# Regrouped first loads and an earlier start of pair 0 in an attention and mixture-of-experts kernel

## Chip, cores and metric

The kernel runs on one core of one Trainium2 chip. The metric is the device time of one execution in microseconds; the median of several executions is compared.

## What is computed

Four batches of eight heads of causal attention over 768 tokens with head size 64, and on its output a soft mixture of experts with 8 experts of 4 slots each. A head is either a retrieval head (full causal attention) or a streaming head (4 sink tokens and a window of 64); which one it is comes in as data.

```
scores = q @ k.T / 8                            # per batch and head, 768 x 768
keep   = causal & (retrieval | sink | window)   # sink: column < 4, window: row - column < 64
a      = softmax(where(keep, scores, -1e9));  x = a @ v
x      -> (3072, 512)                           # tokens x (heads * head size)
logits = x @ phi                                # 3072 x 32 slots
slot_input = softmax over tokens(logits).T @ x
slot_out[e] = relu(slot_input[e] @ w1[e]) @ w2[e]     # 512 -> 1024 -> 512, 8 experts
out    = softmax over slots(logits) @ slot_out  # 3072 x 512, float32
```

## The kernel before

The attention part works on 16 pairs of heads, numbered n = 0 to 15: pair n is heads 2(n mod 4) and the next one of batch n // 4. The schedule is written out by hand: each engine runs its instructions in the order of the program, and waits by semaphore for what they need.

**One pair.** `load` (L70) brings q, k and v with a cast from float32 to bfloat16, 96 partitions with 8 rows of 64 each. `transpose` (L80) turns each with 16 PE transposes into PSUM, `evac` (L89) copies that to SBUF (pair 0's q on ACT, all others on DVE); for v a second set of transposes, `v_blocks`, and `evac_blocks` build the layout for the second product. The causal scores are cut into six groups, g = 0 to 5 (`GROUPS`, L23). For each, `qk` (L113) makes the scores on PE and the exponential on ACT; `mask` (L134) multiplies groups 0 to 2 by the head's mask on DVE; the sink and window rule of groups 3 to 5 is a bias (`fb0`, `fb1`) inside the exponential. `pvmm` (L145) multiplies by v on PE, `norm` divides on DVE. Two PSUM tiles hold scores at a time. While pair n is in groups 2, 3 and 4, the q, k and v of pair n + 1 are transposed and copied. `x_transpose`, `token_logits`, `exp_tokens`, `exp_slots` and `dispatch` do the routing of a batch while the next batch's attention runs.

**Raw tiles.** The q, k and v that were loaded wait in memory that belongs to the last three experts' second weights (`at.late = w2s[NE - 3:]`). `raw_tile` (L64) gives pair n its place: four places each for q, k and v, two couples of pairs. A load into a place must wait until PE has transposed what lies there, and those last weights must wait until pair 15 has been transposed.

**Loads.** GpSimd (POOL) issues nearly all of them on one queue, q0, in the order of the program: k and v of pair 0, q, k, v of pair 1, and q, k, v of pairs 2 and 3 in one load each; then, in the loop, one weight matrix of 1 MB per pair (none where n mod 4 is 3), and for odd n q, k, v of pairs n + 3 and n + 4. Behind n = 13 the rest follows: the last two second weights come in four halves of 512 KB, because the end is cut in two halves of the output's columns. q of pair 0 comes as float32 over SP and is cast by DVE and ACT (L368, L369).

**Start of pair 0.** Behind a few constants come the transposes of q and k with zero matmuls between them (`warm`, L58), whose results are not used. Then DVE reads the heads' flags (`rne`, `r1`, `r0`, L377 to L379) and makes the masks: `head_mask(h)` (L381) writes the mask of one head in two instructions. Heads 0 and 1 are made inside pair 0's group 0, the others at the places of `MASK_AT` (L33).

**End.** `layer1` makes the hidden layer of four experts at a time, `layer2(e, c0, cl)` (L543, matmul in L547) adds one expert's output, on half the columns for the last two experts. `row_sums(b)` (L240) makes the softmax's divisor of a batch. `slot_cols` (L572) scales, and `piece` (L580) makes and stores the output: first the first half of the columns for batches 0 and 1, then the second half, then batches 2 and 3 whole. Ahead of the expert layers five small loads on SP write a few values of `moe_phi` into the mask of head 7, which nothing reads any more (L480 to L482).

Of the kernel before, what the change touches and what calls it, by code (L numbers as in the profile page):

```python
# [10 lines left out]
F32 = mybir.dt.float32  # L11
BF16 = mybir.dt.bfloat16
I32 = mybir.dt.int32
ALU = mybir.AluOpType
# [15 lines left out]
MCOL = [0, None, 256]  # L30
NG = len(GROUPS)

MASK_AT = {(0, 2): 2, (0, 3): 3, (0, 4): 4, (1, 1): 5, (1, 2): 6, (1, 3): 7}  # L33


class Attn:
# [26 lines left out]

    def raw_tile(self, w, n):  # L64

        t = self.late["qkv".index(w)].rearrange("p (i h a) d -> p i h (a d)", i=2, h=4)[:, n // 2 % 2]
        self.rawt[w, n] = t[:, 2 * (n % 2):2 * (n % 2) + 2]
        return t

    def load(self, n, which="qkv", pairs=1):  # L70
        b, h = n // 4, 2 * (n % 4)
        for w in which:
            for m in range(n, n + pairs):
                t = self.raw_tile(w, m)
            c = 2 * (n % 2)
            self.nc.gpsimd.dma_start(  # L76
                t[:96, c:c + 2 * pairs],
                self.src[w][b, h:h + 2 * pairs].rearrange("h (p s) d -> p h (s d)", s=8))

    def transpose(self, n, w):  # L80
        src = self.rawt[w, n]
# [7 lines left out]
    def evac(self, n, w):  # L89
        tp = self.tp.pop((w, n))  # L90
        pool = self.vTp if w == "v" else self.qkT
        dst = pool.tile([P, 768], BF16, tag=w + "T", name=w + "T")
        o = dst.rearrange("c (j s p) -> c j s p", j=6, s=8)
        i = tp.rearrange("c (s j p) -> c j s p", j=6, s=8)
        if n == 0 and w == "q":
            self.nc.scalar.copy(o, i)
        else:
            self.nc.vector.tensor_copy(o, i)  # L98
        self.T[w, n] = dst
# [150 lines left out]
def kernel(  # L250
# [13 lines left out]
    nc = tc.nc  # L264
    B, H, S, D = q.shape
    n_sink, window = int(n_sink), int(window)
    ES = moe_phi.shape[1]
    NE, DM, F = moe_w1.shape
    SPE = ES // NE
    NP = B * H // 2  # L270
# [26 lines left out]
    fb0 = singles.tile([P, H], F32, name="fb0")  # L297
    fb1 = singles.tile([P, H], F32, name="fb1")
# [4 lines left out]
    with ExitStack() as actx:  # L303
# [5 lines left out]
        msk = asing.tile([P, H, 640], BF16, name="msk")  # L309
        ri = asing.tile([P, 2 * H], I32, name="ri")  # L310
        rne = asing.tile([P, H, 2], F32, name="rne")
        r1 = asing.tile([P, H], F32, name="r1")
        r0 = asing.tile([P, H], F32, name="r0")
# [8 lines left out]
                   fb0=fb0, fb1=fb1, vbufs=vbufs, scale=1.0 / (D ** 0.5))  # L322
        ir32 = is_retrieval.tensor.reshape([H]).bitcast(I32)
        at = Attn(nc, tc, actx, q, k, v, env)
# [14 lines left out]
        nc.gpsimd.memset(ident, 1.0)  # L339
        nc.gpsimd.affine_select(ident, ident, pattern=[[-1, P]], compare_op=ALU.is_equal,  # L340
                                fill=0.0, base=0, channel_multiplier=1)
        at.load(1)
        at.load(2, pairs=2)

        for vb in vbufs:
            nc.vector.memset(vb[:, :, :, 64:65], 1.0)
# [23 lines left out]
        at.transpose(0, "q")  # L370
        at.warm(4, 512)
        at.evac(0, "q")
        at.transpose(0, "k")
        at.warm(3, 512)
        at.evac(0, "k")

        nc.vector.tensor_single_scalar(rne, ri.rearrange("p (h c) -> p h c", c=2), 0.0, op=ALU.not_equal)  # L377
        nc.vector.tensor_tensor(r1, rne[:, :, 0], rne[:, :, 1], op=ALU.max)
# [2 lines left out]
        def head_mask(h):  # L381
            for c0, c1, r in ((0, 256, r0), (256, 640, r1)):
                nc.vector.tensor_scalar(msk[:, h, c0:c1], level[:, c0:c1], r[:, h:h + 1], 2.0,
                                        op0=ALU.add, op1=ALU.is_ge)

        for n in range(NP):
            if n % 2 and n + 3 < NP:
                at.load(n + 3, pairs=2)
            for _ in range(0 if n % 4 == 3 or n > 13 else len(w_order) - 5 if n == 13 else 1):
                w_load(*w_order.pop(0))  # L390
            if n == 1:

                nc.gpsimd.memset(sum4, 1.0)
                for g in range(4):
                    nc.gpsimd.affine_select(sum4[32 * g:32 * (g + 1)], sum4[32 * g:32 * (g + 1)],
                                            pattern=[[-1, ES]], compare_op=ALU.is_equal,
                                            fill=0.0, base=0, channel_multiplier=1)
                phf = at.small.tile([P, 4, ES], F32, tag="eb", name="phf", bufs=1)
                nc.sync.dma_start(phf, moe_phi.rearrange("(do di) s -> di do s", di=P))
            for g in range(NG):  # L400
                at.qk(n, g)
                last = n == NP - 1

                b, bt = (n - 4) // 4, (n - 4) % 4 if n >= 4 else 0
                if g == 0:
                    if n == 0:
                        at.transpose(0, "v")
                        at.warm(3)
                        head_mask(0)
                        at.evac(0, "v")  # L410
                        head_mask(1)


                        nc.vector.tensor_scalar(fb0, r0, 1.0, 30000.0, op0=ALU.subtract, op1=ALU.mult)
                        nc.vector.tensor_scalar(fb1, r1, 1.0, 30000.0, op0=ALU.subtract, op1=ALU.mult)
                    else:
                        at.pvmm(n - 1, 4)
                        at.v_blocks(n)
                        at.evac_blocks(n)
                    at.mask(n, 0)  # L420
                elif g == 1:
                    if n:
                        at.pvmm(n - 1, 5)
                    else:
                        at.v_blocks(n)
                        at.evac_blocks(n)
                    if bt == 2:
                        at.exp_slots(b, 0)
                    elif bt == 3:
                        at.dispatch(b, slot_bf if last else None)  # L430
                    if n:
                        at.norm(n - 1, 1)
                elif g == 2:
                    if not last:
                        at.transpose(n + 1, "q")
                    at.pvmm(n, 0)
                    at.mask(n, 1)
                    if not last:
                        at.evac(n + 1, "q")
                elif g == 3:  # L440
                    if not last:
                        at.transpose(n + 1, "k")
                    at.pvmm(n, 1)
                    at.mask(n, 2)
                    if not last:
                        at.evac(n + 1, "k")
                elif g == 4:
                    if not last:
                        at.transpose(n + 1, "v")
                    at.pvmm(n, 2)  # L450
                    if not last:
                        at.evac(n + 1, "v")
                    if bt == 2:
                        at.exp_slots(b, 1)
                elif g == 5:
                    if n:
                        at.x_transpose(n - 1)
                    at.pvmm(n, 3)
                    if n:
                        at.evac_x(n - 1)  # L460
                    at.norm(n, 0)
                if n == NP - 2 and g == NG - 1:
                    for w in w_order:
                        w_load(*w)
                if n == 0 and g < 3:
                    at.warm(4)
                if bt == 1 and g in (0, 3):
                    at.token_logits(b, g // 3)
                    at.exp_tokens(b, g // 3, nc.vector if b == B - 2 else nc.gpsimd)
                if (n, g) in MASK_AT:  # L470
                    head_mask(MASK_AT[n, g])
                if n == 2 and g == 0:
                    nc.vector.tensor_copy(phi, phf)
                if n == 3 and 2 <= g:
                    gg = g - 2
                    for e4 in range(2):
                        s0 = SPE * (4 * e4 + gg)
                        nc.vector.reduce_sum(emask[32 * gg:32 * (gg + 1), e4:e4 + 1],
                                             sum4[32 * gg:32 * (gg + 1), s0:s0 + SPE], axis=AX.X)
        dead = msk[:, H - 1, :].bitcast(F32)  # L480
        for j, (rows, cols) in enumerate(((8, 10), (4, 11), (2, 12), (12, 9), (1, 13))):
            nc.sync.dma_start(dead[:rows, 16 * j:16 * j + cols], moe_phi[:rows, :cols])  # L482
        n, b = NP - 1, B - 1
        at.pvmm(n, NG - 2)

# [57 lines left out]
        def layer2(e, c0=0, cl=DM):  # L543
            e4, g = e // 4, e % 4
            for fo in range(8):
                r = fo % 4
                nc.tensor.matmul(sp[32 * r:32 * (r + 1), c0:c0 + cl], hT[e4][:, fo, 32 * g:32 * (g + 1)],  # L547
                                 w2s[e][:, fo, c0:c0 + cl], start=(e == 0 and fo < 4),
                                 stop=(e == NE - 1 and fo >= 4), skip_group_check=True)
# [16 lines left out]
        h_transpose(1, 1)  # L566
        for e in range(2, NE - 2):
            layer2(e)
        for b in range(2):
            at.row_sums(b)  # L570

        def slot_cols(c):  # L572

            nc.scalar.activation(slot_out[:, 256 * c:256 * (c + 1)], sp[:, 256 * c:256 * (c + 1)], ACT.Copy, scale=rcol)  # L574
# [20 lines left out]
            nc.sync.dma_start(ov[:, r:r + m, c0:c0 + cl], ot[:, o:o + m, c0:c0 + cl])  # L595

        HALF = DM // 2
        for e in (NE - 2, NE - 1):
            layer2(e, 0, HALF)
        slot_cols(0)  # L600
        for b, r, m in ((0, 0, 1), (0, 1, 2), (0, 3, 3), (1, 0, 3), (1, 3, 3)):
            piece(b, r, m, 0, HALF)
# [45 lines left out]
```

## Time and profile before

| | |
|---|---|
| median of 4 runs | 152.02 us (151.64 to 152.58) |
| profiled execution, its own time | 152.98 us |
| its span, first to last instruction | 151.3 us |
| PE, DVE, ACT, POOL busy | 130.1, 116.3, 113.3, 33.6 us |
| q0 (GpSimd's loads) | 26.02 MB, 94.5% of the span |
| HBM read, written | 52.50 MB, 6.29 MB |

The profile is of one execution. Engines: PE is TensorE's matmuls and PEld its weight loads, DVE is VectorE, ACT ScalarE, POOL GpSimd, SP SyncE. In the page, slices are fortieths of the span and a digit is the busy share in tenths. In lists of instructions a line gives start, duration, engine, line of the code, operation, output<-input, shapes, count, and in brackets the idle time before it with what ended that. L76 is the load of q, k or v, L279 and L281 that of a first or second weight matrix, L85 a transpose, L98 its copy to SBUF, L121 scores, L126 and L130 exponentials, L140 and L143 masks, L156 the product with v, L61 a zero matmul.

### The profile page before, as it was taken

The page shows a single profiled execution, that of the slowest core. Times are in us where ns is not written, and L with a number is a line of the kernel's source. Part 1 is how long each engine was busy: PE and PEld are TensorE (multiplying, and loading weights), DVE is VectorE, ACT ScalarE, POOL GpSimd, SP SyncE. Part 2 cuts the span into 40 slices and gives each one's busy share as a digit, 9 for nine tenths or more (in the row PEclk, how much of TensorE's full clock was granted, in tenths as well). Part 3 has the DMA queues.
Part 4 walks back from the last instruction along what each step waited for, and adds up shares of the span by engine and source line. Part 5 has one row for each costly group of instructions (what it writes and reads, how often), then busy time and mean ns, then how long its engine had stood idle before and what let it go on. Part 6 is the DMA issues. An engine that isn't in the chain of part 4 may idle for free.

```text
span 151.3 us, 5526 instructions
## 1 busy us (share of the span) xinstructions
PE 130.1 (86%) x2377; PEld 84.7 (56%) x2377; DVE 116.3 (77%) x289; ACT 113.3 (75%) x181; POOL 33.6 (22%) x61
## 2 busy tenths in 40 slices
PE   6699988998999899999989999998979997839700
PEld 2257656765677566677766667676556354614200
DVE  6199999899897999889799898989965341708900
ACT  3347989999899898999989899998981440718800
POOL 7913801401422330152235010005400000000000
PEclk9999999999999999999999999999999999975865
DMA  4999999999999999999999999999999999987995
GB/s 109 138 194 207 225 200 210 224 214 199 212 226 195 214 217 219 198 209 227 196 213 224 214 200 212 225 212 214 217 214 217 195 197 200 208 295 235 377 416 237
DMA packets 20381, 33.12 MB, mean 219 GB/s; under 512 B 1670, under 2 KB 17862, under 8 KB 18566
## 3 DMA queue, kind: packets, MB, share of 16 engines
q0 software_dynamic: 15616, 26.02, 94.5%
q1 hardware_dynamic: 4742, 6.76, 12.7%
q8 instruction: 18, 0.29, 0.7%
q14 instruction: 5, 0.04, 0.1%
HBM read 52.50 MB, written 6.29 MB: 389 GB/s over the span
## 4 chain that ended last, share of the span: by engine, by line
DMA 34%; PE 28%; DVE 26%; issue 2%; ACT 2%; POOL 1%; DVEq 0%; POOLq 0%
DMA w<-in_moe_w_dram 18%; DMA w<-in_v_dram 12%; PE pv L156 6%; DVE xb L169 6%; PE sc L121 6%; DVE pT L143 4%; PE tpv L85 4%; DMA w<-in_k_dram 4%; PE op L589 4%; DVE pT L140 4%; DVE vb L110 3%; DVE xT L183 3%; PE tpx L177 2%; PE waste L61 2%; DVE rs L167 1%
## 5 line engine op out<-in xcount | busy, mean ns | idle before, releaser
L130 ACT ACTIVATE pT<-sc,fb 128x512 bf16<-128x512 f32 (+1 forms) x96 | 52.0, 616 | 5.1 <-PE sc L121 4.2
L126 ACT ACTIVATE pT<-sc 128x1024 bf16<-128x1024 f32 (+1 forms) x48 | 44.4, 952 | 5.6 <-PE sc L121 4.1
L156 PE MATMUL pv<-vb,pT 128*128 128x65 bf16 x672 | 37.1, 195 | 5.2 <-DVE pT L140 3.8
L156 PEld LDWEIGHTS <-pT 128*128 128x128 bf16 x672 | 26.3, 97 | 16.4 <-issue 6.3
L121 PE MATMUL sc<-qT,kT 64*128 64x256 bf16 (+3 forms) x320 | 35.0, 281 | 0.2
L85 PEld LDWEIGHTS <-w 96*64 96x64 bf16 x768 | 19.2, 110 | 11.9 <-issue 8.0
L143 DVE TENSOR_TENSOR pT<-pT,msk 128x1024 bf16<-128x1024 bf16 (+1 forms) x32 | 19.7, 616 | 0.0
L169 DVE TENSOR_TENSOR xb<-pv,rs 128x384 bf16<-128x384 f32 x32 | 17.8, 557 | 1.1
L121 PEld LDWEIGHTS <-kT 64*128 64x128 bf16 x320 | 10.7, 94 | 8.0 <-issue 1.9
L594 DVE TENSOR_SCALAR w<-op,rrow 128x256 f32<-128x256 f32 (+1 forms) x18 | 9.5, 570 | 6.9 <-PE op L589 6.6
L183 DVE COPY xT<-tpx 128x768 bf16<-128x768 bf16 (+1 forms) x17 | 9.1, 534 | 5.7 <-PE tpx L177 5.5
L76 POOL DMA_DIRECT2D w<-in_q_dram x8 | 5.5, 689 | 35.4 <-PE tpq L85 30.8
L281 POOL DMA_DIRECT2D w<-in_moe_w_dram x10 | 6.7, 676 | 21.6 <-PE tpq L85 14.3
L98 DVE COPY kT<-tpk 128x768 bf16<-128x768 bf16 x16 | 8.8, 551 | 3.2 <-PE tpk L85 3.2
L140 DVE TENSOR_TENSOR pT<-pT,msk 128x1024 bf16<-128x1024 bf16 x16 | 10.9, 682 | 0.0
L589 PE MATMUL op<-slot_out,expT 128*128 128x256 bf16 (+1 forms) x36 | 9.5, 390 | 1.5 <-ACT slot_out L574 1.1
L592 ACT ACTIVATE w<-op,rrow 128x256 f32<-128x256 f32 (+1 forms) x18 | 9.1, 543 | 1.5 <-PE op L589 1.4
L61 PE MATMUL waste<-zeros 128*128 128x256 bf16 (+1 forms) x39 | 8.9, 356 | 1.3 <-DVE zeros L337 1.3
L98 DVE COPY vT<-tpv 128x768 bf16<-128x768 bf16 x16 | 8.8, 552 | 1.4 <-PE tpv L85 1.3
L85 PE MATMUL tpk<-ident,w 96*64 96x96 bf16 x256 | 8.5, 209 | 1.0 <-DMA w<-in_k_dram 1.0
L110 DVE COPY vb<-tpb 128x768 bf16<-128x768 bf16 x16 | 8.9, 557 | 0.2 <-PE tpb L104 0.2
L85 PE MATMUL tpq<-ident,w 96*64 96x96 bf16 x256 | 8.5, 210 | 0.3 <-DVE w L368 0.3
(85 smaller groups left out, 144.5 us busy)
## 6 DMA issues: line engine op xcount, KB each, us to landing
w<-in_moe_w_dram POOLq DMA_DIRECT2D x14, 1024.0 KB, 20.6
out_dram<-w SPq DMA_DIRECT2D x4, 768.0 KB, 4.0
w<-in_q_dram POOLq DMA_DIRECT2D x7, 384.0 KB, 14.9
w<-in_k_dram POOLq DMA_DIRECT2D x7, 384.0 KB, 15.6
w<-in_v_dram POOLq DMA_DIRECT2D x7, 384.0 KB, 16.2
out_dram<-w SPq DMA_DIRECT2D x6, 384.0 KB, 3.6
w<-in_moe_w_dram POOLq DMA_DIRECT2D x4, 512.0 KB, 24.1
out_dram<-w SPq DMA_DIRECT2D x2, 256.0 KB, 4.9
```

The costliest lines, as they stand in the source:

```text
L85: self.nc.tensor.transpose(tp[64 * i:64 * (i + 1), s * 96:(s + 1) * 96], src[:96, i, s * 64:(s + 1) * 64], self.ident[:96, :96])
L98: self.nc.vector.tensor_copy(o, i)
L110: self.nc.vector.tensor_copy(self.vbufs[n % 2][:, :, :, :64], tp.rearrange("p (j h d) -> p h j d", j=6, h=2))
L121: nc.tensor.matmul(sc[:, hh, c:c + ni * P], kT[po:po + 64, j * P:(j + 1) * P], qT[po:po + 64, i0 * P:(i0 + ni) * P], start=True, stop=True)
L126: nc.scalar.activation(pT[:, :, :L], sc[:, :, :L], ACT.Exp, scale=self.scale)
L130: nc.scalar.activation(pT[:, hh, :L], sc[:, hh, :L], ACT.Exp, scale=self.scale, bias=fb[:, h + hh:h + hh + 1])
L140: nc.vector.tensor_mul(v, v, m)
L143: nc.vector.tensor_mul(pT[:, :, :L], pT[:, :, :L], self.msk[:, h:h + 2, c:c + L])
L156: self.nc.tensor.matmul(self.pv[n, lo][:, hh, i % 3, :], pT[:, hh, o:o + P], vb[:, hh, j, :65], start=first, stop=True, skip_group_check=True)
L169: nc.vector.tensor_mul(xo, pv[:, :, :, :64], rs.to_broadcast([P, 2, 3, 64]))
L183: self.nc.vector.tensor_copy(self.xT[n // 4][:, n % 4, c], self.tp.pop(("x", n))[:, c])
L589: nc.tensor.matmul(op[:, :cl], er[:, r + i, :], slot_out[:, c0:c0 + cl], start=True, stop=True)
```

## The change

q and k are moved by one pair against v: the couples of q and k are now (1, 2), (3, 4), ..., (13, 14) and 15 alone, those of v stay (2, 3), ..., (14, 15). q and k of pairs 1 and 2 come in one load each right behind k and v of pair 0, then v of pair 1, then v of pairs 2 and 3. In the loop q and k are loaded at even n, v at odd n. The flags and the masks of heads 0 and 1 are made ahead of the transposes of pair 0's k; the copy of that k is made in two parts; the biases and the mask of head 2 follow it, and the other masks move by one place. The second group of pair 0's scores comes right behind the first. Zero matmuls in pair 0's groups fall from 3 + 4 + 4 + 4 to 2 + 2. The five small loads into head 7's mask go, and the row sums of batches 0 and 1 move behind the first half of expert 6.

```diff
-MASK_AT = {(0, 2): 2, (0, 3): 3, (0, 4): 4, (1, 1): 5, (1, 2): 6, (1, 3): 7}
+MASK_AT = {(0, 2): 3, (0, 3): 4, (0, 4): 5, (1, 1): 6, (1, 2): 7}
...
     def raw_tile(self, w, n):
-        t = self.late["qkv".index(w)].rearrange("p (i h a) d -> p i h (a d)", i=2, h=4)[:, n // 2 % 2]
-        self.rawt[w, n] = t[:, 2 * (n % 2):2 * (n % 2) + 2]
-        return t
+        m = n + (w != "v")
+        t = self.late["qkv".index(w)].rearrange("p (i h a) d -> p i h (a d)", i=2, h=4)[:, m // 2 % 2]
+        self.rawt[w, n] = t[:, 2 * (m % 2):2 * (m % 2) + 2]
+        return t, 2 * (m % 2)
...
     def load(self, n, which="qkv", pairs=1):
-        b, h = n // 4, 2 * (n % 4)
         for w in which:
-            for m in range(n, n + pairs):
-                t = self.raw_tile(w, m)
-            c = 2 * (n % 2)
+            for m in range(n + pairs - 1, n - 1, -1):
+                t, c = self.raw_tile(w, m)
             self.nc.gpsimd.dma_start(
                 t[:96, c:c + 2 * pairs],
-                self.src[w][b, h:h + 2 * pairs].rearrange("h (p s) d -> p h (s d)", s=8))
+                self.src[w].rearrange("b h (p s) d -> p (b h) (s d)", s=8)[:, 2 * n:2 * (n + pairs)])
...
         if n == 0 and w == "q":
             self.nc.scalar.copy(o, i)
+        elif n == 0 and w == "k":
+            for c in (slice(0, 2), slice(2, 6)):
+                self.nc.vector.tensor_copy(o[:, c], i[:, c])
...
-        at.load(1)
-        at.load(2, pairs=2)
+        at.load(1, "qk", 2)
+        at.load(1, "v")
+        at.load(2, "v", 2)
...
         at.evac(0, "q")
-        at.transpose(0, "k")
-        at.warm(3, 512)
-        at.evac(0, "k")
...
+        head_mask(0)
+        head_mask(1)
+        at.transpose(0, "k")
+        at.warm(3, 512)
+        at.evac(0, "k")
+        nc.vector.tensor_scalar(fb0, r0, 1.0, 30000.0, op0=ALU.subtract, op1=ALU.mult)
+        nc.vector.tensor_scalar(fb1, r1, 1.0, 30000.0, op0=ALU.subtract, op1=ALU.mult)
+        head_mask(2)

         for n in range(NP):
-            if n % 2 and n + 3 < NP:
-                at.load(n + 3, pairs=2)
+            if n + 3 < NP:
+                at.load(n + 3, "v" if n % 2 else "qk", min(2, NP - n - 3))
...
             for g in range(NG):
-                at.qk(n, g)
+                if n or g != 1:
+                    at.qk(n, g)
+                if n == 0 and g == 0:
+                    at.qk(n, 1)
...
                     if n == 0:
                         at.transpose(0, "v")
-                        at.warm(3)
-                        head_mask(0)
                         at.evac(0, "v")
-                        head_mask(1)
-                        nc.vector.tensor_scalar(fb0, r0, 1.0, 30000.0, op0=ALU.subtract, op1=ALU.mult)
-                        nc.vector.tensor_scalar(fb1, r1, 1.0, 30000.0, op0=ALU.subtract, op1=ALU.mult)
...
-                if n == 0 and g < 3:
-                    at.warm(4)
+                if n == 0 and g < 2:
+                    at.warm(2)
...
-        dead = msk[:, H - 1, :].bitcast(F32)
-        for j, (rows, cols) in enumerate(((8, 10), (4, 11), (2, 12), (12, 9), (1, 13))):
-            nc.sync.dma_start(dead[:rows, 16 * j:16 * j + cols], moe_phi[:rows, :cols])
...
-        for b in range(2):
-            at.row_sums(b)
...
-        for e in (NE - 2, NE - 1):
-            layer2(e, 0, HALF)
+        layer2(NE - 2, 0, HALF)
+        for b in range(2):
+            at.row_sums(b)
+        layer2(NE - 1, 0, HALF)
         slot_cols(0)
```

## Prediction

> **What bounds the kernel now.** I read the page first: span, the slices, the queues, the chain. Its lines:
>
> ```profile
> span 151.3 us, 5526 instructions
> ...
> DMA  4999999999999999999999999999999999987995
> ...
> q0 software_dynamic: 15616, 26.02, 94.5%
> q1 hardware_dynamic: 4742, 6.76, 12.7%
> ...
> HBM read 52.50 MB, written 6.29 MB: 389 GB/s over the span
> ```
>
> The DMA row is at 9 from the second slice to the end of the inputs, and one queue, q0 (GpSimd's loads of q, k, v and the expert weights, cast from float32 to bfloat16 on the way), makes nearly all of it. PE, DVE and ACT are busy too (86, 77 and 75%), so the shares alone do not name the bound. The chain of waits in order of time does (start, duration, what):
>
> ```profile
> 79.32 18.66 DMA w<-in_v_dram
> ...
> 106.03 0.86 POOL w L281
> 106.89 27.46 DMA w<-in_moe_w_dram
> 134.39 0.64 PE sp L547 x8
> 135.05 0.48 ACT slot_out L574
> 135.58 5.54 PE op L589 x18
> ```
>
> The last transfer of the weights is issued at 106.89 us and lands at 134.35, 27.46 later, though it is only 512 KB: it stands behind a queue. Then the waits of the stretch 113 to 152 us and PE's timeline there:
>
> ```profile
> PE sp L547 <- DMA w<-in_moe_w_dram: 2.8, 2, 1.8
> ```
> ```profile
> 112.16 0.87 PE L156 MATMUL pv<-vb,pT 128*128 128x65 bf16 x16
> ...
> 126.65 0.40 PE L547 MATMUL sp<-w,hT 128*32 128x256 bf16 x8
> 128.00 0.40 PE L547 MATMUL sp<-w,hT 128*32 128x256 bf16 x8 [0.95 <-DMA w<-in_moe_w_dram]
> ...
> 134.39 0.62 PE L547 MATMUL sp<-w,hT 128*32 128x256 bf16 x8 [1.82 <-DMA w<-in_moe_w_dram]
> ```
>
> Attention's last products are at 113 us. The expert layers follow without a stop until PE waits 0.95 us for the first half of the last expert's second matrix, and 1.82 us for its second half. So attention has a slack of 0.95 + 1.82 = 2.77 us: what it gains becomes waiting at these two places, what it loses up to 2.77 us is taken from them. Behind 134.39 the tail is 151.3 - 134.39 = 16.9 us, output alone.
>
> Last, engine use in stretches (busy us and count of PE, PEld, DVE, ACT, POOL; then granted clock, DMA share, GB/s), for the start and for the end of the queue:
>
> ```profile
> 5.00:10.00 5.00, 3.99 (x62) 2.15 (x58) 2.08 (x8) 1.82 (x2) 2.96 (x5) 1.00 1.18 178
> 10.00:15.00 5.00, 5.00 (x100) 3.37 (x98) 4.84 (x15) 3.56 (x6) 1.41 (x2) 1.00 1.23 204
> ...
> 125.00:130.00 5.00, 3.24 (x54) 2.06 (x47) 0.99 (x4) 1.19 (x3) 0.00 (x0) 1.00 1.37 186
> 130.00:135.00 5.00, 3.10 (x36) 1.90 (x35) 2.31 (x7) 1.79 (x5) 0.00 (x0) 0.94 1.04 298
> 135.00:140.00 5.00, 4.43 (x18) 2.22 (x17) 3.31 (x7) 4.04 (x9) 0.00 (x0) 0.50 0.67 222
> ```
>
> A share over 1 means overlapping packets: the queue holds work throughout. It carries 26.02 MB from about 3.9 us (first packet) to 134.35, 199 GB/s written, twice that read. Is that a rate an edit can raise? The Trainium skill ("DMA: Bandwidth & Descriptors", Specifications) gives two ceilings: 435 GB/s into SBUF and about 358 GB/s of HBM per core. By the first alone q0 needs 26.02 / 0.435 = 60 us (an estimate), transfers would hide, and attention would set the end. The row decides for the other side: about 52 MB read in 130.5 us is 399 GB/s, already above the page's HBM figure. So I take the stream as full: its end moves with its first packet, its bytes, or a time without work.
>
> **The change, part by part.**
>
> *Loads.* Before, GpSimd issues 2 loads (k, v of pair 0), 3 for pair 1, and 3 for each of seven couples of pairs: 26. After: k and v of pair 0, then q12, k12, v1, v23 (4), then q and k at n = 0, 2, ..., 12 (14) and v at n = 1, 3, ..., 11 (6): again 26, with the same bytes and pieces, at the page's 0.67 to 0.69 us of POOL each. Cost to the stream 0, if the queue never runs dry. POOL's order: q34 needs pair 0's q transposes (5.2 us: no wait), k34 needs its k transposes (end 7.77), and the first weight now stands behind that: issue near 8.5 in place of 7.48. v45 and the second weight then wait for pair 1's v transposes, near 14. Issued by 9 us: 2 x 0.197 + 2 x 0.393 + 0.197 + 0.393 + 2 x 0.393 + 1.049 = 3.6 MB; at the rows' 178 to 204 GB/s some 1.8 MB have moved by 14. So 1.8 MB, 9 us, cover that wait. Later POOL waits at n for transposes of n - 1, as before. The last five weight issues wait for pair 15's v transposes (104.50 in the trace), with 12 us of queue still ahead of them: cover again, worth up to 12 us if it were gone.
>
> Arrival: k of pair 1 now has 1.18 MB up to and with it (before 0.79), v 1.38 (before 0.98): about 2 us later each, near 12.7 and 13.7 us. PE took them at 13.16 and 14.29 and will ask some 0.5 to 1 us sooner; so 0 to 0.5 us of waiting at the start. Later v comes 0.39 MB, 1.9 us, sooner in the queue; q and k of pairs 13 and 14 are the tightest (42 and 44 loads of 0.197 MB and 8 weights up to and with them: 16.65 and 17.04 MB, at the mean rate 87.3 and 89.3 us, wanted about 1 us sooner than PE's 88.78 and 90.14). Loss some 0.2 us, at most 0.5, within the slack.
>
> *Flags and masks.* Three flag operations (0.17 + 0.17 + 0.23) and masks of heads 0 and 1 (0.52 + 0.51) move ahead of k's copy. DVE is idle 3.17 us before that copy at 7.81, and the flags' load lands 3.8 us after its issue at 1.26. Flags and masks then end near 5.1 + 1.6 = 6.7, before the k transposes do: cost 0. If the flags came over 1 us later, k's copy, queued behind on DVE, would be late, and everything after it. Gain on DVE after 8.3 us: 1.6 us.
>
> *Copy of k in two.* 0.56 us becomes two copies. Upper bound: two whole rows, +0.56; lower bound: -0.3, if the first scores could start after a third of it. Nearest rows, 256-column DVE operations at 0.26: +0.1. On the path nothing: PE's three filler matmuls run to 8.52 anyway, and the chain before names them as what the first scores follow.
>
> *Second scores at once.* ACT was idle 0.63 us before the second exponential (10.55); it now follows the first at 9.91. Gain 0.6 us there.
>
> *Fillers.* 7 + 4 + 4 zero matmuls of 256 columns (0.94 + 0.60 + 0.60 us) become 2 + 2: a saving of PE work, about 1.6 us, some of which was waiting. Here a rule speaks against the change: the Trainium skill ("TensorE: Matmul & The Clock Gate", HAM oscillation, and Part 4) says that a window of 3.4 us without enough PE work halves the clock, and that transposes do not count as such work in the same way. Row: granted clock 1.00 in every stretch from 5 to 130 us, then 0.50 in 135 to 140, after a stretch with 1.82 us of waiting. By the rule pair 0, now mostly transposes between 8.5 and 12 us, could lose its clock for a window or two: 3.4 us each at half speed, 1.7 us of work lost each. By the row, attention with its many transposes keeps full clock: 0. I take the row; even two windows lose 3.4, less 2.77 slack and 1 of head start: nothing.
>
> *Five small loads into dead mask space, removed.* 1.61 us of SP queue at 111.07, and SP's next work is at 129.78: 0. *Row sums of batches 0 and 1* (12 matmuls, 0.72 us at 126.00) move behind one half of expert 6: hidden by the 0.95 us wait that follows in either order.
>
> **Sum.** Attention ends 0.5 to 1.6 us sooner, 1 in the middle. What is late next: the same weight halves, at 128.0 and 134.35. PE's waits grow from 2.77 to nearly 4 us. Profiled execution: 134.39 + 16.9 = 151.3 of span, and 152.98 with 1.7 outside; change 0. That execution lies 0.96 above the median of the four runs, 152.02, so the forecast is 152.0.
>
> **Rivals.** (1) *Attention, not the stream, sets the end* and passes its gain on: 152.0 - 1 to 1.6, about 150.7. For it: busy engines. Against it: both DMA waits. 0.08. (2) *The last transfer lands elsewhere.* The packet records show the 16 engines of q0 ending between 129.6 and 134.34, fourteen of them by 131.95; the last halves share those engines with the first outputs. Another order of loads, or the small loads' absence, could shift that straggler: up to 2.4 us sooner, or later by a like amount. Typical 1 us: 151.0 (0.11) or 153.1 (0.09). (3) *The early clock drop, slower:* place 8.5 us on, price 1.7 us a window; it decides only from 2.77 + 1.0 + 0.76 = 4.5 us lost, three windows: 152.0 + 5.1 - 3.8 = 153.3. 0.06. (4) *The queue runs dry* in POOL's wait near 14 us: each idle us counts fully; it needs 9 us of cover gone: 153.5. 0.02. (5) That the change doesn't do what it says: the waits named for POOL are real, so the loads do come in this order. If merging did nothing, still no change.
>
> **How the numbers follow.** No change 0.64, its own range 151.3 to 152.75; faster 0.08 + 0.11 = 0.19; slower 0.09 + 0.06 + 0.02 = 0.17. The bound is 0.5%, 0.76 us, about what a measurement of this kernel can tell from no change. For 8 in 10 the range reaches to about 151.0 minus a little and 153.1: 150.8 to 153.1.
>
> **What would show it.** Right: the last weight landing near 134.3; q0 at about 94%; attention's end near 112; the two waits of L547 grown to about 4 us in sum; DVE idle before k's copy shrunk from 3.17 to near 1; no ACT gap before the second exponential. Wrong: L547 without waits and an end that moved with attention (1); a landing moved by over 0.8 us with no idle slice (2); a granted clock below 1 before 20 us (3); a DMA row below 9 early (4).

## The result and the profile after

The changed kernel takes 152.47 us (median of 44 runs, 151.47 to 153.32), the kernel before 151.89 us (63 runs, 151.28 to 153.3): a ratio of 1.0035, 95% interval 1.0023 to 1.0047. So the change costs about 0.5 us. It lies within the 0.76 us that the prediction called no change, but it is a loss and not nothing, and the prediction had named no step that would cost it. The profiled execution of the changed kernel took 152.58 us, its span is 150.9 us; single executions of either kernel differ by 2 us, so the two profiles' totals (150.9 against 151.3) say nothing on which is slower. They are read for places, not for sums.

The page of the changed kernel: span, DMA share in fortieths of the span, the queue of GpSimd's loads.

```profile
span 150.9 us, 5498 instructions
...
DMA  4999999999999999999999999999999999997994
...
q0 software_dynamic: 15616, 26.02, 94.8%
```

The same packets and bytes, and no slice without work. The chain of waits (start, duration, what) ends as before:

```profile
105.89 27.77 DMA w<-in_moe_w_dram
133.66 0.04 issue
133.70 0.64 PE sp L552 x8
```

L552 is the matmul of `layer2`, L547 before. PE's timeline of the same kernel near the end, and its engine use by stretches (busy us and count of PE, PEld, DVE, ACT, POOL; granted clock, DMA share, GB/s):

```profile
125.41 0.40 PE L552 MATMUL sp<-w,hT 128*32 128x256 bf16 x8 [0.36 <-DMA w<-in_moe_w_dram]
...
128.06 0.40 PE L552 MATMUL sp<-w,hT 128*32 128x256 bf16 x8 [1.59 <-DMA w<-in_moe_w_dram]
...
132.43 0.62 PE L552 MATMUL sp<-w,hT 128*32 128x256 bf16 x8
133.70 0.62 PE L552 MATMUL sp<-w,hT 128*32 128x256 bf16 x8 [0.65 <-DMA w<-in_moe_w_dram]
```
```profile
125.00:130.00 5.00, 2.24 (x38) 1.67 (x34) 0.94 (x4) 1.13 (x3) 0.00 (x0) 1.00 1.35 184
130.00:135.00 5.00, 3.71 (x37) 2.25 (x36) 2.51 (x7) 2.52 (x6) 0.00 (x0) 0.52 1.05 299
135.00:140.00 5.00, 5.00 (x18) 2.35 (x18) 3.89 (x8) 4.12 (x8) 0.00 (x0) 0.50 0.81 271
```

PE waits 0.36 + 1.59 us before 128 us, where it waited 0.95 before the change: that is the head start of attention, whose last products with v start 1.0 us sooner in this pair of profiles. First before, then after:

```profile
113.85 0.28 PE L156 MATMUL pv<-vb,pT 128*128 128x65 bf16 x4
```
```profile
112.84 0.29 PE L158 MATMUL pv<-vb,pT 128*128 128x65 bf16 x4
```

But the granted clock is 0.52 in 130 to 135, where it was 0.94, and the same matmuls then take 0.62 in place of 0.40 us. PE is ready for the last half 0.5 us later than before, and in this execution it lands 0.7 us sooner (133.66 in place of 134.35), so that the last wait shrinks from 1.82 to 0.65.

The start went as predicted. DVE waits 0.85 us for the k transposes in place of 3.17, and ACT runs the first two exponentials back to back (x2, no idle time between), where the second had 0.63 us of idle time ahead of it. Before, then after:

```profile
7.81 0.56 DVE L98 COPY kT<-tpk 128x768 bf16<-128x768 bf16 x1 [3.17 <-PE tpk L85]
```
```profile
10.55 1.96 ACT L126 ACTIVATE pT<-sc 128x1024 bf16<-128x1024 f32 x2 [0.63 <-PE sc L121]
```

```profile
7.61 0.62 DVE L98 COPY kT<-tpk 128x256 bf16<-128x256 bf16 x2 [0.85 <-PE tpk L84]
```
```profile
8.69 1.94 ACT L128 ACTIVATE pT<-sc 128x1024 bf16<-128x1024 f32 x2 [2.13 <-PE sc L123]
```

What the prediction did not look at is SP. Its waits in the whole span (us in total, times, longest) have one line for the waits that close the program; first before, then after:

```profile
SPq L643 <- DMA out_dram<-w: 5.2, 3, 1.9
```
```profile
SPq L647 <- DMA out_dram<-w: 5.4, 1, 5.4
```

Before, SP waits for landings of the output three times, one behind the other as the stores land; after, once, for 5.4 us, and that is for the last store. The records of SP's instructions behind it show why that costs. The program closes with eight waits on SP, one for each completion semaphore that its transfers take in turn, always in the same order and about 60 ns apart. Below, by the numbers of the semaphores, are the wait that ended with the last store's landing and those behind it, each with its place in us against the end of the span:

```
before   S116 -1.022   S117 -0.963   S118 -0.901   then the closing handshake of the engines
after    S101 -1.326   S103 -1.265   S113 -1.205   S114 -1.144   S115 -1.085   S116 -1.023   S117 -0.964   S118 -0.902
```

Transfer number m on SP takes place m mod 8 in this list of eight (101, 103, 113 to 118), the eighth where m divides by 8. Before there are 3 loads, 5 small loads and 14 stores, 22 transfers, so the last store has the sixth semaphore. Without the small loads there are 17, and it has the first: seven more waits must be passed after it has landed, not two. The difference is 1.326 - 1.022 = 0.30 us. The chain of waits doesn't show it, since it is followed back from the last instruction of an engine's own work.

### The profile page after: what moved, and what is told of

The parts are those of the page before. It is cut to its first block, busy times and chain, and to the rows that moved or that the text cites. A ratio compares the mean times of both kernels' runs of the same rounds, so it can differ in the third digit from the quotient of the medians.

```text
span 150.9 us, 5498 instructions
## 1 busy us (share of the span) xinstructions
PE 129.1 (86%) x2366; PEld 84.1 (56%) x2366; DVE 116.8 (77%) x290; ACT 113.4 (75%) x181; POOL 33.7 (22%) x61
## 4 chain that ended last, share of the span: by engine, by line
PE 36%; DVE 28%; DMA 24%; POOL 3%; issue 2%; ACT 1%; DVEq 0%; POOLq 0%
DMA w<-in_moe_w_dram 18%; PE pv L158 10%; PE sc L123 8%; DVE xb L171 7%; DMA w<-in_k_dram 5%; PE tpv L84 4%; DVE pT L145 4%; DVE pT L142 4%; DVE vb L112 4%; PE op L591 4%; PE tpx L179 4%; DVE xT L185 3%; PE tpk L84 2%; DVE rs L169 1%; PE lt L197 1%
## 5 line engine op out<-in xcount | busy, mean ns | idle before, releaser
L145 DVE TENSOR_TENSOR pT<-pT,msk 128x1024 bf16<-128x1024 bf16 (+1 forms) x32 | 19.7, 616 | 0.0
L75 POOL DMA_DIRECT2D w<-in_v_dram x9 | 6.0, 669 | 34.9 <-PE tpv L84 34.9
L84 PE MATMUL tpv<-ident,w 96*64 96x96 bf16 x256 | 8.5, 209 | 0.1
L61 PE MATMUL waste<-zeros 128*128 128x512 bf16 (+1 forms) x28 | 7.4, 383 | 1.3 <-DVE zeros L339 1.3
```

The source lines that it names most:

```text
L84: self.nc.tensor.transpose(tp[64 * i:64 * (i + 1), s * 96:(s + 1) * 96], src[:96, i, s * 64:(s + 1) * 64], self.ident[:96, :96])
L145: nc.vector.tensor_mul(pT[:, :, :L], pT[:, :, :L], self.msk[:, h:h + 2, c:c + L])
```

## The experiments

Theory 1 blames the new order of loads, theory 2 the removed small loads (the semaphore above), theory 3 the moved row sums, theory 4 the earlier start.

**Each part alone.** Four kernels, each the kernel before with one part of the diff.

Loads only (`raw_tile`, `load`, the first loads, the loop's load line; here two pieces):

```diff
...
+        m = n + (w != "v")
...
-        at.load(1)
-        at.load(2, pairs=2)
+        at.load(1, "qk", 2)
+        at.load(1, "v")
+        at.load(2, "v", 2)
```

> Before with the regrouped loads alone. Theory 1 (the new order of loads lengthens the stream of q0 or moves its last landing): +0.4 to +0.6 us against before, as the whole change. Theory 2 (absence of the five small loads), 3 (row sums moved, PE clock in the tail) and 4 (the earlier start of pair 0): 0 +- 0.15 us.

Measured: 152.0 us against 151.77, ratio 1.0018 (0.9999 to 1.0036).

Small loads removed only:

```diff
-        dead = msk[:, H - 1, :].bitcast(F32)
-        for j, (rows, cols) in enumerate(((8, 10), (4, 11), (2, 12), (12, 9), (1, 13))):
-            nc.sync.dma_start(dead[:rows, 16 * j:16 * j + cols], moe_phi[:rows, :cols])
```

> Before without the five small loads into head 7's mask, nothing else changed. Theory 2 (the small loads shift which engines or completion slots the output stores use, and the tail is longer without them): +0.4 to +0.6 us. Theories 1, 3 and 4: 0 +- 0.15 us.

Measured: 152.18 us, ratio 1.0022 (1.0003 to 1.0042), 0.33 us. In its profile the last store's wait is the first of the eight, 1.325 us from the end.

Row sums moved only:

```diff
-        for b in range(2):
-            at.row_sums(b)
...
+        layer2(NE - 2, 0, HALF)
+        for b in range(2):
+            at.row_sums(b)
+        layer2(NE - 1, 0, HALF)
```

> Before with the row sums of batches 0 and 1 moved behind the first half of expert 6, nothing else changed. Theory 3 (the tail's order and clock): +0.3 to +0.6 us. Theories 1, 2 and 4: 0 +- 0.15 us, since 0.7 us of row sums move within a wait for the weights.

Measured: 151.84 us, ratio 0.9998 (0.9986 to 1.0010).

Earlier start only (the other hunks: `MASK_AT`, k's copy in two, masks and flags ahead, second scores at once, fewer zero matmuls):

```diff
...
+        head_mask(0)
+        head_mask(1)
+        at.transpose(0, "k")
...
```

> Before with the earlier start of pair 0 alone (flags and masks ahead of k, k's copy in two, second scores at once, fewer zero matmuls). Theory 4 (attention that ends sooner leaves PE waiting longer at the end, at half clock, or issues its last weights so that they land later): +0.3 to +0.6 us. Theories 1, 2 and 3: 0 +- 0.15 us, the gain being lost in the wait for the weights.

Measured: 151.89 us, ratio 1.0001 (0.9983 to 1.0019).

So theories 3 and 4 fall as causes by themselves; what is left of the loss stands on two parts, each near the edge of what such a comparison resolves: 0.18% for the loads and 0.22% for the small loads, together 0.40% where the whole change measures 0.35%.

PE's waits of the earlier start alone, in 88 to 110 us (us in total, times, longest), show that it needs the new order of loads:

```profile
PE tpk L85 <- DMA w<-in_k_dram: 0.7, 1, 0.7
PE pv L159 <- DVE pT L143: 0.5, 1, 0.5
PE tpv L85 <- DMA w<-in_v_dram: 0.4, 1, 0.4
```

Under the old order pair 14's k and v land just in time for the old start, so attention loses its head start there and its last products start at 113.85 us as before. In the changed kernel these two waits are gone.

**Theory 2, by dose.** The changed kernel with small loads put back, five and three of them; the diff is the three removed lines again, for three with a shorter list. And the opposite way: no small load, the loads' order of before, the first two stores made one, so that SP has 16 transfers and the last store the eighth semaphore.

```diff
-        for b, r, m in ((0, 0, 1), (0, 1, 2), (0, 3, 3), (1, 0, 3), (1, 3, 3)):
+        for b, r, m in ((0, 0, 3), (0, 3, 3), (1, 0, 3), (1, 3, 3)):
             piece(b, r, m, 0, HALF)
```

> The changed kernel with the five small loads put back. In the traces so far SP ends with eight waits, one for each completion semaphore of its queue, 60 ns apart; the last store's semaphore is the first of them where the small loads are gone (1.35 us from its landing to the end) and the sixth where they are there (1.02 to 1.08). Theory 2 (small loads only turn that order): the stretch from the last store's landing to the end back at 1.05 us, time -0.3 us against the changed kernel, so +0.1 to +0.25 us against before (what the loads' order leaves). If the small loads do nothing (theory 1 alone): stays at +0.5 us.

> The changed kernel with three of the five small loads. Theory 2: the last store has the fourth semaphore of eight, so from the last landing to the end 1.36 - 3 x 0.06 = 1.18 us. If only the presence of small loads matters: 1.05 us; if they do nothing: 1.36 us.

> The changed kernel with the loads' order of before, without small loads, and with the first two stores of the first half made one: 13 stores + 3 loads = 16 transfers on SP, so the last store has the eighth semaphore, the last one waited for. Theory 2: 0.90 to 0.95 us from the last landing to the end, and -0.1 us against before (0 to -0.3). If the semaphore's place doesn't matter: 1.35 us as without small loads, and +0.3 us.

The wait that ends with the last store's landing, and its time to the end, from the records of SP:

| kernel | transfers on SP | semaphore of the last store | to the end |
|---|---|---|---|
| changed | 17 | first | 1.326 us |
| changed, three small loads | 20 | fourth | 1.143 us |
| changed, five small loads | 22 | sixth | 1.022 us |
| 16 transfers | 16 | eighth | 0.901 us |

Each place is 0.060 us, and the presence of small loads as such does nothing. Theory 2 had asked for 1.18, 1.05 and 0.90 to 0.95 us from the landing itself to the end; so counted it is 1.16, 1.04 and 0.92. In time, five small loads gave 152.01 us, ratio 1.0011 (0.9993 to 1.0029); the 16 transfers 151.89 us, 1.0001 (0.9980 to 1.0021), so its expected 0.1 us under before can't be told; three small loads have one run, 152.61 us, which says nothing on a tenth.

Both kernels were run once more side by side:

> The changed kernel once more, beside its variants. If the last store's semaphore accounts for 0.30 us of it and something else for the rest: +0.45 to +0.6 us against before.

> The changed kernel with the five small loads once more: 0.30 us under the changed kernel if the semaphore's place is all that they do (+0.15 to +0.3 us against before). If the rest is noise: +0 us.

Measured: changed 152.43 us, ratio 1.0034 (1.0013 to 1.0056); with five small loads 152.05 us, 1.0018 (0.9998 to 1.0038). Over all runs of this study the means are 151.92 us before (280 runs, standard error 0.03), 152.45 changed (66 runs, 0.06) and 152.12 with the small loads back (44 runs, 0.07). The small loads are worth 0.33 +- 0.09 us, as the 0.30 of the records says. The rest, 152.12 - 151.92 = 0.20 +- 0.07 us, has another cause. (Each set of runs against the runs of before that were measured beside it: 0.53 and 0.53 us, and 0.16 and 0.21.)

**Is the stream the bound, and how much slack is there?** The load of expert 7's first weights is left out, in three kernels; expert 6's are used in its place, so these kernels leave out a part of the work and compute a wrong output.

```diff
-    w_order = [(i,) for i in range(2 * NE - 2)] + [
+    w_order = [(i,) for i in range(2 * NE - 2) if i != 7] + [
...
-                                     w1s[4 * e4 + g][:, do, c * 512:(c + 1) * 512],
+                                     w1s[min(4 * e4 + g, 6)][:, do, c * 512:(c + 1) * 512],
```

> Before without the load of expert 7's first weights (1 MB; the hidden layer uses expert 6's in its place, so one expert's output is of the wrong weights). One weight takes 4.9 us of the stream. If the stream sets the end with a slack of attention of 1 to 2.8 us behind it: -1 to -2.8 us, then attention sets the end. If attention had no slack: 0. If it had more slack than 4.9 us: -4.9 us.

Measured: 149.79 us, ratio 0.9862 (0.9840 to 0.9884): 2.1 us less. PE's timeline has no wait for weights any more, and both experts' halves follow each other at once (x16):

```profile
126.64 0.62 PE L547 MATMUL sp<-w,hT 128*32 128x256 bf16 x16
...
131.03 0.62 PE L547 MATMUL sp<-w,hT 128*32 128x256 bf16 x16
```

One weight is 4.9 us of stream, but only 2.1 us come out, then attention sets the end. The slack that the prediction read off (2.77 us in one execution) is of this size.

> The same, with the earlier start of pair 0. If the stream hides that start's gain in the full kernel: here, where attention sets the end, it is worth 0.5 to 1 us against the kernel without that load. If the earlier start gains nothing by itself: 0.

Measured: 149.31 us, ratio 0.9843 (0.9823 to 0.9863). With four runs each this is not told from the kernel without the earlier start. Its profile shows attention stopped for k and v at pair 14 as in the earlier start alone, and the last half at 130.93.

> The changed kernel without the load of expert 7's first weights (expert 6's are used in its place, so one expert's output is of the wrong weights). In the kernel before without that load attention sets the end (149.8 us, -1.4% against before), and with the earlier start under the old order of loads attention gave 0.9 us back at pair 14, where k and v came late. If the new order is what lets attention keep its head start: attention ends 1 us sooner, about 149.1 us (0.3 us of the 1 lost to the last store's semaphore); if the head start is worth nothing even where attention sets the end: 149.8 to 150.1 us.

Measured: 149.14 us, ratio 0.9813 (0.9764 to 0.9863). The interval is wide (four runs); the timelines are clearer, though each is of one execution:

```profile
125.85 0.40 PE L552 MATMUL sp<-w,hT 128*32 128x256 bf16 x8
...
130.02 0.62 PE L552 MATMUL sp<-w,hT 128*32 128x256 bf16 x16
```

130.02 against 131.03: the head start is worth 1.0 us in this pair where attention sets the end, and 130.93 against 131.03 says that it needs the new order of loads. Of the 1.0 us, 0.3 go again at the end (spans 147.4 and 148.1 us). In the full kernel the stream hides all of it.

**What in the order of loads?** Two kernels change how often the stream goes from pieces of 1 KB (q, k, v) to pieces of 8 KB (weights). What is measured is the stretch of q0 between the packets whose ends complete 1.0 and 19.7 MB: all of q, k, v and ten weights. Counted so, it comes out about 0.1 us shorter than the figures of earlier profiles in the first of the two expectations.

The new order of loads in the kernel before, and the weights two at a time:

```diff
...
-            for _ in range(0 if n % 4 == 3 or n > 13 else len(w_order) - 5 if n == 13 else 1):
+            for _ in range(len(w_order) - 5 if n == 13 else 0 if n % 2 or n > 13 else 1 + (n % 4 == 2)):
                 w_load(*w_order.pop(0))
```

> Before with the new order of loads, but the weights two at a time at n = 2, 6, 10 and one at 0, 4, 8, 12, so that the stream changes between pieces of 1 KB and of 8 KB as often as before (7 stretches of small pieces in place of 10). In the packet records, from 1.0 MB to 19.7 MB (all of q, k, v and ten weights) the order of before takes 90.02 to 90.08 us and the new order 90.10 to 90.23. If the changes between sizes cost it: 90.05. If the order or grouping of q, k and v does: 90.2.

Measured: 151.96 us, ratio 0.9989 (0.9968 to 1.0010); 90.45 us for that part of the stream. So here the new order of loads costs nothing against before.

The old order, with a weight between q and k:

```diff
             if n % 2 and n + 3 < NP:
-                at.load(n + 3, pairs=2)
+                at.load(n + 3, "q", 2)
+                w_load(*w_order.pop(0))
+                at.load(n + 3, "kv", 2)
-            for _ in range(0 if n % 4 == 3 or n > 13 else len(w_order) - 5 if n == 13 else 1):
+            for _ in range(len(w_order) - 5 if n == 13 else 1 if n == 0 or n in (2, 6, 10) else 0):
```

> Before with its order of q, k and v, but a weight between q and k of each couple: 11 stretches of small pieces in place of 7. If changes between sizes cost the stream: 90.2 to 90.3 us from 1.0 MB to 19.7 MB. If not: 90.05. The time against before: +0.2 us by the first, 0 by the second, too small to be told from 0 with certainty.

Measured: 89.75 us for that part of the stream, and 154.82 us in all, ratio 1.0178 (1.0132 to 1.0224). More changes between sizes don't lengthen the stream: the kernel with most of them has the shortest stretch, the one with few the longest. The time, expected within 0.2 us of before, was a miss of another kind. PE's waits behind 15 us:

```profile
PE tpk L85 <- DMA w<-in_k_dram: 2.5, 2, 2.2
PE pv L156 <- DVE pT L140: 2.2, 6, 0.5
PE tpv L85 <- DMA w<-in_v_dram: 0.7, 1, 0.7
```

A weight ahead of k lets k land 4.9 us of stream later, and PE waits 2.2 us for it, until 47.36 us. Behind that wait the granted clock is at half from 47.8 to 54.6 us, which makes attention later still (four matmuls of scores take 0.61 in place of 0.39 us): its last products start at 118.66 us, 4.8 later than before and past the slack, and PE has no wait for weights left. The order of loads can cost much, through attention; in the changed kernel it doesn't by this way, since there attention ends sooner.

Over all profiles of the full stream, the stretch from 1.0 to 19.7 MB takes 89.89 to 90.03 us in the old order (mean 89.98 of seven, the split one apart) and 89.93 to 90.09 in the new (mean 90.02 of eight, the grouped one apart): 0.04 us, too little for what is sought.

**Theory 5: the clock in the tail.** The head start lengthens PE's wait before 128 us, and this may lower the clock. The granted clock, averaged over the span and all runs, is 0.953 in the changed kernel and 0.960 before. In a second profile of the changed kernel the half clock came at 127.8 us and PE itself got late: no wait is left before the last half.

```profile
128.06 0.62 PE L552 MATMUL sp<-w,hT 128*32 128x256 bf16 x8 [1.60 <-DMA w<-in_moe_w_dram]
...
132.84 1.18 PE L552 MATMUL sp<-w,hT 128*32 128x256 bf16 x16
```

What half clock costs can be read from the landing of the last half matrix to the end of the span, in all 16 profiles of the full stream but the split one. Two things sort them: the semaphore of the last store, and how long the last eight matmuls of `layer2` take.

| semaphore of the last store | eight matmuls in 0.40 us | in 0.62 us (half clock) |
|---|---|---|
| first | 16.97 us | 17.20, 17.21 |
| fourth | | 17.04 |
| sixth | 16.67 to 16.72 (five profiles) | 16.91 to 16.94 (four, the kernel before among them) |
| eighth | 16.50 to 16.56 (three) | |

Half clock at that place costs 0.24 us and the first semaphore in place of the sixth 0.30; half clock behind it costs nothing that shows (136.0 to 139.4 us in the second profile with five small loads, which has 16.68). So in this stretch the clock can make a difference between the kernels only by how often it is at half for those eight matmuls. That the head start is what lowers it is not shown: in the profile of the loads alone PE waits for weights 0.9 us in sum, and half clock lasts from 129.7 to 140.0; the mean clock is 0.958 with the loads alone and 0.956 in the grouped kernel, both with the old start, and 0.958 with the earlier start alone.

The waits were then filled with zero matmuls, in four kernels: the changed kernel with small loads, the one with 16 transfers, the kernel before (6 in place of 10), and the changed kernel with 16 transfers.

```diff
+        at.warm(10)
         layer2(NE - 1, 0, HALF)
...
-        for e in (NE - 2, NE - 1):
-            layer2(e, HALF, HALF)
+        layer2(NE - 2, HALF, HALF)
+        at.warm(5)
+        layer2(NE - 1, HALF, HALF)
```

> The same with 10 and 5 zero matmuls in PE's two waits for the last expert's halves. Theory 5 (what is left, some 0.2 us, comes from the head start: PE waits longer before 128 us, the granted clock falls to half for 10 us in place of 7 and PE's own work in the tail gets late): mean granted clock up from 0.951 to 0.96 or more, and 0.1 to 0.25 us faster than without them. Theory 1 (the order of loads): no change in time, whatever the clock does.

> The kernel with the loads' order of before, 16 transfers on SP and the earlier start, with the same zero matmuls. Theory 5: 0.1 to 0.25 us under the one without (which was level with before), so -0.2 us against before. If the clock doesn't matter: level with before or 0.1 us under it.

> Before with 6 and 5 zero matmuls in PE's two waits for the last expert's halves. Zero matmuls there took 0.27 and 0.25 us off the two kernels with the earlier start. If the half clock is a cost of the earlier start's longer waits: before, whose granted clock is higher to begin with (0.960 against 0.952), gains 0.15 us or less. If it gains 0.25 us too, the earlier start has no part of its own in the clock's cost, and the rest of 0.2 us stays open.

> The changed kernel (its order of loads, no small loads) with the first two stores of the first half made one, so that the last store has the eighth semaphore, and 10 and 5 zero matmuls in the two waits: differs from the fastest kernel so far (151.55 us, 0.9975 of before) in the order of loads alone. If the order of loads costs nothing: 0.9975 +- 0.0015 of before. If it costs 0.1 to 0.2 us: 0.998 to 0.999.

| kernel | without fillers, ratio to before | with fillers | mean clock without, with |
|---|---|---|---|
| changed, five small loads | 1.0018 (0.9998 to 1.0038) | 0.9992 (0.9967 to 1.0016) | 0.952, 0.975 |
| earlier start, old order, 16 transfers | 1.0001 (0.9980 to 1.0021) | 0.9975 (0.9958 to 0.9992) | 0.955, 0.979 |
| before | 1 | 0.9993 (0.9972 to 1.0015) | 0.960, 0.972 |
| changed, 16 transfers | not run | 0.9992 (0.9975 to 1.0009) | -, 0.978 |

The stretches of the second row's kernel with fillers show the clock held through the last halves:

```profile
130.00:135.00 5.00, 3.69 (x43) 2.60 (x42) 2.04 (x7) 2.11 (x6) 0.00 (x0) 1.00 1.07 304
135.00:140.00 5.00, 4.48 (x21) 2.27 (x19) 4.85 (x10) 4.90 (x11) 0.00 (x0) 1.00 0.89 302
```

Fillers bring 0.26% in both kernels with the earlier start and 0.07% in the kernel before. All these intervals overlap, so that a part of the clock's cost is the head start's own is not shown. With clock and last semaphore held alike, the new order of loads (fourth row) is 0.17% behind the old one (second row), again with overlapping intervals. This agrees with the loads alone (0.18%), but not with the grouped kernel (-0.11%).

One sum over all runs of these kernels says more than any pair. Take the twelve kernels of the full stream (the split one and the single run apart) with the kernel before of each set of runs, and let the parts add up. The best fit gives 0.36 +- 0.06 us to the first semaphore in place of the sixth, 0.15 +- 0.06 to the new order of loads, 0.02 +- 0.06 to the earlier start and -0.20 +- 0.08 to the fillers (standard errors). So the remaining 0.20 us go with the order of loads more likely than with the head start. How that order costs them is open: not by changes of piece size, hardly by the rate of the stream (0.04 us), not by a later attention; half clock more often at the last halves (five of seven profiles without fillers in the new order, two of five in the old) would fit, and so would a later last landing (means 133.5 and 133.4 us, each profile between 132.7 and 134.4), but neither is shown.

One kernel is faster than before and than the changed one: the second row with fillers, 151.55 us, 0.9975 (0.9958 to 0.9992) of before. It has the earlier start, the old order of loads, 16 transfers on SP and the fillers.

## Why the prediction was right and wrong

- *The bound.* Right. q0 sets the end; without one weight 2.1 us come off and PE's waits for weights vanish. The slack of 2.77 us was read from one execution; PE's two waits at the same places differ by profile (their sum is 0.9 us in the profile of the loads alone), so it should have been given as a range.
- *Flags and masks, copy of k, second scores.* Right in size and in worth: attention ended 1.0 us sooner, as the middle of its range said, and the time gained nothing. A part of that number is luck, since single executions differ in when k arrives. From the first transpose of k to the last product with v it is 106.9 us in five profiles of the old start, and 106.0 to 106.6 in seven of eight with both the earlier start and the new loads (107.5 in the eighth, where pair 1's q and k came late): 0.3 to 0.9 us gained.
- *What is late next.* Half right. The next wait is for the same weight halves, but their sum is 2.60 us (0.36 + 1.59 + 0.65), not nearly 4. The prediction let the clock stay as it was. In the changed kernel's profile the half clock came 4 us earlier, at 130.2 in place of 134.4 us, and the slower work of PE took 0.5 us of the difference; the other 0.7 us are the earlier landing of the last half in that execution.
- *The rule on the clock.* The Trainium skill's rule ("TensorE: Matmul & The Clock Gate", HAM oscillation) was weighed at the start alone. There nothing happened in the changed kernel (granted clock 1.00 in every stretch from 5 to 130 us), as the row had said. In the grouped kernel, with the old start and all its zero matmuls, the clock was at half from 7.8 to 11.2 us and attention took 108.4 us, and its time shows no loss: PE's waits for weights absorbed it (0.5 us in sum are left of them). At the end the clock fell to 0.52 behind 2.24 us of PE work in 125 to 130. The page's "no PE-idle gaps >~3.4µs" would have let it stand there, since the longest gap was 1.59 us; the measurement decides.
- *Loads.* "Cost to the stream 0, if the queue never runs dry": the queue didn't run dry, and the stretch of the stream is the same within 0.04 us. Still some 0.15 to 0.2 us hang on this part by the runs. Not explained.
- *Five small loads removed: "SP's next work is at 129.78: 0".* This is the step that failed. The prediction asked whom the small loads delay, and nobody is delayed. It did not ask what counts them. They shift which semaphore the last store gets, and SP's closing waits pass that semaphore first: 0.30 of the 0.53 us. The other 0.2 us have no shown cause; by the runs they go with the loads, which the prediction put at 0 too.
- *Tail: "151.3 - 134.39 = 16.9 us, output alone".* It was taken as fixed. The last 1.0 to 1.3 us of it are no output but SP's waits and the closing handshake, and the change reached into them.
- *Rivals.* None of them named the cause. The second, a last transfer that lands elsewhere, has no support at the size that it was given: the last weights land between 132.7 and 134.3 us in the old order and between 132.9 and 133.9 in the new. A shift of 0.2 us would not be seen in this spread.

## What to carry to other kernels

When a transfer is removed or added, ask not only what it delays but what it numbers: completion semaphores are handed out in turn, and the one that the last store gets decides how many closing waits lie behind its landing. A head start ahead of a full transfer queue becomes waiting and is worth nothing; cheap matmuls in the wait kept the clock up and were worth some 0.2 us over four kernels. Differences of a few tenths in a kernel whose runs spread over 2 us have to be sought in records that repeat exactly, as the 60 ns steps and the stretch behind the last landing did, and not in the totals of single profiles.

## What was not expected of the hardware

Eight waits on SP for semaphores that are already there take 0.060 us each, to within 2 ns in every profile: 0.42 us between the best and the worst place of the last store. The granted clock fell to half behind waits that look short: 0.36 and 1.59 us, with 2.2 us of PE work in 5 us, in the changed kernel; 0.9 us in sum, with 3.6 us of PE work in 5 us, with the loads alone. In all profiles the drops ahead of the final one lasted 3.41, 6.83 or 10.24 us, never another length. In attention, where PE also runs many transposes, the clock stayed at 1.00 in the profiles before and after; one wait of 2.2 us there, in the split kernel, brought half clock for 6.8 us.
